# A fused attention and two expert layers on one core: the first loads on two queues, fewer warm products, and another split of the last accumulators

## The chip, the core and the metric

The kernel runs on one core of a Trainium2 chip. A core has TensorE (PE, with its weight loads shown apart as PEld), VectorE (DVE), ScalarE (ACT), GpSimd (POOL) and SyncE (SP), and 16 DMA engines. Here SP and ACT start transfers: SPq and ACTq in the rows below. The metric is the device time of one execution in microseconds (us).

## The reference, cut to what matters

```python
def _attn_ref(q, k, v, tau):            # q, k, v: 4 x 8 x 576 x 64, float32
    scores = scale * np.matmul(q, k.transpose(0, 1, 3, 2))
    thresh = np.max(scores, axis=-1, keepdims=True) - tau
    scores = np.where(scores >= thresh, scores, -1000000000.0)
    ...
    attn = attn / (np.sum(attn, axis=-1, keepdims=True) + 1e-09)
    return np.matmul(attn, v)
# x: the attention's output as 2304 x 512
h = x @ w_in;  r = np.maximum(h, 0.0);  x = (s * (r * r) + b) @ w_out                   # layer one, 512 -> 2048 -> 512
h = x @ w_in;  return (np.maximum(h, 0.0) + alpha * np.minimum(h, 0.0)) @ w_out         # layer two, same sizes
```

## The kernel before, in words

The attention works on pairs of heads: 16 pairs, of which the first four (`p < NP`) are done with plain float32 products and the others with split operands. For each pair, two heads of q, k and v are brought into tiles called `nat` (three of them, used in turn) and `v32`, 128 rows by 4 blocks for the main part of one head (128 KB, the function `load`, L667), and for the last 64 of the 576 rows a small transfer for both heads, the tail (32 KB, L684 and L686). The tail of k and the tail of q of one pair lie in the same tile `nat["k"]`, in its fifth block: k in partitions 0 to 63, q in 64 to 127. PE turns `nat` by transposes (L317 and L319) into a PSUM bank; ACT copies turned k to `k32` (L726), DVE and ACT write the scaled q of either head to `q32` (L738, L740; the first pair's lies in the tile `gw`); PE multiplies them to scores (L804, tile `sc`, two of them); DVE takes the row maximum (L814, `mx`), POOL the threshold (L816), ACT the exponential (L818) and DVE the masked product with its sum (L820, `e`). Then e is turned and multiplied with v.

The order on each engine is not written by hand. Every piece of work is a task with an engine (or several to choose from), a cost, its reads and writes as `Buf` objects, and a rank; `Plan.run` walks through a modelled time and gives each free engine the ready task of lowest rank. What it emits is one fixed list per engine, and the instructions' own semaphore waits are put in afterwards, by tile. So a change of one cost or rank at the start can reorder everything behind it. Layer one is mixed in with the attention by the same ranks; its weights are brought and rebuilt by DVE, ACT and POOL meanwhile. The helpers of its products have the lines L541 to L543, three products for each pair of split operands.

`warm` (L902) adds a product of the identity with itself, which nothing reads. `FILL` is their number ahead of the first transposes, `FILLS` the number behind the first pair's transposes, `FILL1` that behind its first scores.

The value `tau` reaches `tau_b` by the first transfer of ACT's queue (L1042); five small DVE instructions make the scales `sc_p`, `by_half` and the threshold `tau_s` of it.

At the end, layer two's output is made in groups of 128 tokens of two blocks by seven products in the order `TURNS` = (1, 2, 5, 6, 3, 7, 4), each over eight steps (the last step of a group: 7 times 6 products, L541 to L543). Their seven accumulators of 256 columns share four PSUM banks, two and two in that order: (1, 2), (5, 6), (3, 7), (4). DVE and ACT then combine them (L1547, L1553, L1557), and `store` writes out (L1565).

## Time and profile before

| | |
|---|---|
| time, median of 3 runs | 1084.25 us (1083.76 to 1086.61) |
| profiled execution: its own time, its span | 1086.08 us, 1084.3 us |
| PE busy, DVE busy, ACT busy, POOL busy | 1054.1, 918.8, 773.6, 374.0 us |
| instructions | 21629 |
| DMA moved | 175.70 MB, mean 162 GB/s |

The span is that from the first to the last instruction; the execution's own time is 1.8 us longer. Times in the rows below count from the span's start. A row of the timeline gives the start, the duration, the engine, the line, the operation with output and inputs, how many were merged into the row, and in brackets how long the engine had been idle and what ended that. A float32 product counts as two instructions there. A busy PE is not a PE at its peak, since overlapping products are merged.

### The profile page before, as it was taken

To read this page: it belongs to the slowest core of one execution; us is meant where nothing else is said; L and a number is where in the kernel's file an instruction comes from. 1 tells how busy PE (TensorE), PEld (TensorE's weight loads), DVE (VectorE), ACT (ScalarE), POOL (GpSimd) and SP (SyncE) were. 2 spreads that over 40 slices of the span, in tenths; PEclk is the share of its full clock that TensorE was granted. 3 is DMA by queue.
4 is the path that set the end of the run, shared out by engine and by line. 5 is a ranking of instruction groups with operands and counts; after the bars stand their busy time and mean duration, and the time that the engine had idled before them with its cause. 6 is when DMAs were issued, how large, how long until landed. Compare 5 with 4: busy or idle time off the path is not lost.

```text
span 1084.3 us, 21629 instructions
## 1 busy us (share of the span) xinstructions
PE 1054.1 (97%) x7022; PEld 1001.0 (92%) x7022; DVE 918.8 (85%) x2089; ACT 773.6 (71%) x1853; POOL 374.0 (34%) x505
## 2 busy tenths in 40 slices
PE   9999889999999999999999999999999999999998
PEld 8767789999898889989999989999999999999998
DVE  5998978998988898958788897798989999998872
ACT  5888867977887788755656685886968996655550
POOL 1566755654674366520100121150102332112110
PEclk9999999999999999999999999999999999999999
DMA  5874464565546653435446976277785564554531
GB/s 131 234 205 124 133 168 113 136 175 135 126 99 167 159 129 93 123 87 169 152 162 225 307 246 197 77 225 242 243 261 203 168 205 147 160 159 121 147 89 39
DMA packets 198385, 175.70 MB, mean 162 GB/s; under 512 B 73600, under 2 KB 176000, under 8 KB 198272
## 3 DMA queue, kind: packets, MB, share of 16 engines
q1 hardware_dynamic: 195968, 172.69, 54.9%
q10 hardware_dynamic: 2304, 1.64, 0.6%
q8 instruction: 55, 0.90, 0.4%
q14 instruction: 58, 0.48, 0.1%
HBM read 100.54 MB, written 50.86 MB: 140 GB/s over the span
## 4 chain that ended last, share of the span: by engine, by line
PE 78%; DVE 5%; DMA 4%; ACT 3%; issue 2%; POOL 1%; SPq 0%; DVEq 0%; ACTq 0%; POOLq 0%
PE bank L541 13%; PE bank L542 12%; PE bank L543 12%; PE bank_b L541 8%; PE bank_b L542 8%; PE bank_b L543 8%; PE bank L926 6%; PE sc L804 6%; PE bank L319 3%; PE bank L317 3%; DMA stg<-in_moe_w_out_dram 3%; DVE e L820 1%; DMA q<-hq 0%; DMA gf<-gw 0%; DVE mx L814 0%
## 5 line engine op out<-in xcount | busy, mean ns | idle before, releaser
L820 DVE SCALAR_TENSOR_TENSOR e<-sc,mx,e 128x576 f32<-128x576 f32 x144 | 116.3, 812 | 15.6 <-ACT e L818 12.5
L814 DVE TENSOR_REDUCE mx<-sc 128x1 f32<-128x576 f32 x144 | 107.0, 749 | 9.2 <-PE sc L804 8.4
L818 ACT ACTIVATE e<-sc,mx 128x576 f32<-128x576 f32 x144 | 106.1, 742 | 10.3 <-DVE mx L814 9.8
L319 PE MATMUL bank<-eyes_r,e 128*128 128x128 f32 (+1 forms) x320 | 89.3, 286 | 0.3 <-ACT e L818 0.3
L541 PE MATMUL bank<-xt,wa 128*128 128x480 f32 (+3 forms) x224 | 83.2, 372 | 6.4 <-ACT gw L1458 2.2
L541 PE MATMUL bank<-gt,wa 128*128 128x384 f32 (+4 forms) x244 | 84.1, 345 | 2.3 <-DVE wa L472 1.5
L542 PE MATMUL bank<-gt,wa 128*128 128x384 f32 (+4 forms) x244 | 81.6, 334 | 0.0
L543 PE MATMUL bank<-gt,wa 128*128 128x384 f32 (+4 forms) x244 | 81.5, 334 | 0.0
L816 POOL TENSOR_SCALAR mx<-mx,tau_s 128x1 f32<-128x1 f32 x144 | 48.0, 334 | 84.0 <-DVE mx L814 79.4
L542 PE MATMUL bank<-xt,wa 128*128 128x480 f32 (+3 forms) x224 | 75.6, 337 | 0.0
L543 PE MATMUL bank<-xt,wa 128*128 128x480 f32 (+3 forms) x224 | 75.5, 337 | 0.0
L926 PE MATMUL bank<-gl,vt 128*128 128x256 f32 (+1 forms) x192 | 65.0, 339 | 0.0
L926 PE MATMUL bank<-gh,vt 128*128 128x256 f32 (+1 forms) x192 | 57.4, 300 | 0.0
L804 PE MATMUL sc<-k,q 128*128 128x288 f32 x264 | 54.5, 334 | 2.8 <-issue 1.7
L984 DVE TENSOR_TENSOR gl<-bank,gh 128x256 fp32r<-128x256 f32 (+1 forms) x96 | 43.4, 452 | 13.0 <-ACT gh L982 11.7
L541 PEld LDWEIGHTS bank<-xt,wa 128*128 128x128 f32 x224 | 43.0, 192 | 11.6 <-ACT rest L572 2.2
L994 POOL TENSOR_TENSOR gr<-gf,gh 64x256 fp32r<-64x256 f32 (+1 forms) x48 | 40.0, 833 | 38.0 <-DVE gl L992 35.1
L541 PEld LDWEIGHTS bank<-gt,wa 128*128 128x128 f32 x244 | 46.5, 190 | 3.4 <-DVE wa L472 1.7
L319 PEld LDWEIGHTS bank<-eyes_r,e 128*128 128x128 f32 (+1 forms) x320 | 44.5, 139 | 5.1 <-ACT e L818 0.5
L543 PEld LDWEIGHTS bank<-gt,wa 128*128 128x128 f32 x244 | 46.0, 189 | 1.6
L982 ACT ACTIVATE gh<-bank 128x256 fp32r<-128x256 f32 (+1 forms) x96 | 39.4, 410 | 11.0 <-PE bank L319 8.8
L542 PEld LDWEIGHTS bank<-gt,wa 128*128 128x128 f32 x244 | 46.1, 189 | 0.5
(734 smaller groups left out, 4206.2 us busy)
## 6 DMA issues: line engine op xcount, KB each, us to landing
stg<-in_moe_w_in_dram SPq DMA_DIRECT2D x32, 512.0 KB, 4.8
stg<-in_moe_w_out_dram SPq DMA_DIRECT2D x32, 512.0 KB, 4.1
gf<-gw SPq DMA_DIRECT2D x41, 192.0 KB, 2.7
q<-hq SPq DMA_DIRECT2D x24, 256.0 KB, 4.1
qo<-hq SPq DMA_DIRECT2D x24, 256.0 KB, 5.1
gw<-gf SPq DMA_DIRECT2D x48, 128.0 KB, 2.9
xt<-xs SPq DMA_DIRECT2D x13, 384.0 KB, 4.9
yat<-ya SPq DMA_DIRECT2D x24, 192.0 KB, 3.5
```

The costliest lines, as they stand in the source:

```text
L319: nc.tensor.transpose(to, part(x), one)
L541: nc.tensor.matmul(o, lhsT=wl, rhs=mh, start=first, stop=False, skip_group_check=on_top)
L542: nc.tensor.matmul(o, lhsT=wh, rhs=ml, start=False, stop=False, skip_group_check=on_top)
L543: nc.tensor.matmul(o, lhsT=wh, rhs=mh, start=False, stop=last, skip_group_check=on_top)
L804: nc.tensor.matmul(sp.t[:, x, :HS], lhsT=o[0][:, c], rhs=o[1][:, x * HS:(x + 1) * HS], start=n == 0, stop=n == len(passes) - 1)
L814: add("DVE", dve(S), lambda sp=sp, mx=mx: nc.vector.tensor_reduce(mx.t[:, 0:1], sp.t[:, :, :HS], op=ALU.max, axis=AX.XY, negate=True), (sp ...
L816: t2 = add("POOL", 0.26, lambda mx=mx: nc.gpsimd.tensor_scalar(mx.t[:, 1:2], mx.t[:, 0:1], -1.0, tau_s, op0=ALU.mult, op1=ALU.subtract), ( ...
L818: add("ACT", act(S, 1), lambda sp=sp, mx=mx, e=e: nc.scalar.activation(halves(e.t), sp.t[:, :, :HS], AF.Exp, bias=mx.t[:, 0:1]), (sp, mx), ...
L820: add("DVE", dve(S) + 0.065, lambda sp=sp, mx=mx, e=e, col=col, sums=sums: nc.vector.scalar_tensor_tensor(halves(e.t), sp.t[:, :, :HS], mx ...
L926: nc.tensor.matmul(o.t[:, :n], lhsT=w.rearrange("p a b -> p (a b)"), rhs=m.t[:, :n], start=c == first and x == 0, stop=c == last and x == ...
L984: add("DVE", dve(n), lambda hi=hi, lo=lo, gt=gt: nc.vector.tensor_tensor(lo.t[:, :n], gt.t[:, :n], f32(hi.t[:, :n]), op=ALU.subtract), (gt ...
L994: add("POOL", pool2(n), lambda hi=hi, f=f, hf=hf: nc.gpsimd.tensor_tensor(hi.t[:TL, :n], f.t[:TL, :n], f32(hf.t[:TL, :n]), op=ALU.subtract ...
```

## The change

It has three parts. The second heads of the first pair's q and k come by ACT's queue, and with them tau moves: its transfer and its five DVE instructions become tasks, the transfer behind these two heads on ACT's queue; k's tail goes over to SP's queue, q's tail stays on ACT's. The tasks of the two tails write a `Buf` of their own (`ending`), so that in the plan the main transposes don't depend on them. The warm products: `FILL` from 12 to 6, and `FILLS` from 3, 2 and 2 to 1, 0 and 2. And the last group of layer two asks for five banks, with another map of products to banks: (1, 2), (5, 6), (3), (7, 4); the fifth `Buf` gets no product and so no bank.

```diff
-FILL, FILL1 = 12, 3
-FILLS = {("k", False): 3, ("k", True): 2, ("q", False): 2}
+FILL, FILL1 = 6, 3
+FILLS = {("k", False): 1, ("k", True): 0, ("q", False): 2}
...
+        def first_consts():
+            x = add("ACT", 0.4, lambda: nc.scalar.dma_start(tau_b, tau.unsqueeze(0).to_broadcast([P, 1])), rank=-LATER, tail=2.2)
+            of_tau.append(add("DVE", 0.9, scales, after=(x,), rank=-LATER))
...
+                    if p == 0 and nm != "v" and h == 1:
+                        add("ACT", 0.66, lambda t=t, src=src: nc.scalar.dma_start(
+                            t.t[:, 0:NQ, 1, :], src[b, h0 + 1, 0:NQ * P, :].rearrange("(p c) d -> p c d", c=NQ)), (), (t,), (), -LATER, wire=wire(128, 256))
+                        if nm == "q":
+                            first_consts()
+                        continue
...
+            ending = Buf()
...
-                        add("ACT", 0.6, lambda t=t, r=r, tl=tl: nc.scalar.dma_start(t.t[r, NQ], tl), (), (t,), (), -LATER, wire=wire(32, 256))
+                        add("SP" if nm == "k" else "ACT", 0.6, lambda t=t, r=r, tl=tl, e=nc.sync if nm == "k" else nc.scalar: e.dma_start(
+                            t.t[r, NQ], tl), (), (ending,), (), asked[nm] if nm == "k" else -LATER, wire=wire(32, 256))
...
-                            add("PE", turned(len(cs)), transpose, (t,), (tr,) if first else (tr, hl), rank=ready)
+                            add("PE", turned(len(cs)), transpose, (t, ending) if tail else (t,), (tr,) if first else (tr, hl), rank=ready)
...
-                acc = [Buf(moe_s) for _ in range(4)]
+                end = i == len(pairs) - 1 and it == TB // P - 1
+                acc = [Buf(moe_s) for _ in range(4 + end)]
...
-                def at(k, acc=acc):
+                def at(k, acc=acc, end=end):
                     x = TURNS.index(k)
+                    x += end and x > 4
                     return acc[x // 2], slice(x % 2 * G1, x % 2 * G1 + G1)
```

The scaling tasks of q also get `after=of_tau`, and the five DVE instructions move into a function `scales`.

Here are rows of ACT's list at the program's start before the change; nat_135 holds the first pair's k and both its tails.

```order
L1042 DMA tau_b<-in_tau_dram 128x1
L684 DMA nat_135<-in_k_dram 64x2x64
L684 DMA nat_135<-in_q_dram 64x2x64
L726 ACT_TABLE_LOAD
L726 ACTIVATE k_181<-bank_109 128x512
L726 ACTIVATE k_181<-bank_112 128x64
L740 ACTIVATE gw_106<-bank_112,by_half 128x64
L740 ACTIVATE gw_106<-bank_109,by_half 128x256
L740 ACTIVATE gw_106<-bank_111,by_half 128x256
```

The same place of ACT's list in the changed kernel; nat_129 is now the tile of k and the tails, nat_131 that of q.

```order
L677 DMA nat_129<-in_k_dram 128x4x64
L677 DMA nat_131<-in_q_dram 128x4x64
L655 DMA tau_b<-in_tau_dram 128x1
L697 DMA nat_129<-in_q_dram 64x2x64
L740 ACT_TABLE_LOAD
L740 ACTIVATE k_175<-bank_109 128x512
L754 ACTIVATE gw_106<-bank_111,by_half 128x256
L754 ACTIVATE gw_106<-bank_110,by_half 128x256
L740 ACTIVATE k_175<-bank_112 128x64
L754 ACTIVATE gw_106<-bank_112,by_half 128x64
```

Two 128 KB transfers stand ahead of tau and of q's tail, and the copy of k's turned tail has moved behind two of q's scalings.

PE's list before, from the last of the nine warm products to the first score, with the semaphores that a row waits for in brackets (DMAHW1, DMAHW2 and so on are those of single transfers).

```order
L902 MATMUL bank_111<-eyes_r 128x128
L317 MATMUL bank_109<-eyes_r,nat0r 128x128 [waits DMAHW3_49,DMAHW4_49,DMAHW2_49,DMAHW1_49]
L317 MATMUL bank_109<-eyes_r,nat0r 128x128 x2
L319 MATMUL bank_109<-eyes_r,nat_135 128x128
L902 MATMUL bank_110<-eyes_r 128x128
L319 MATMUL bank_112<-eyes_r,nat_135 128x128
L902 MATMUL bank_111<-eyes_r 128x128
L902 MATMUL bank_110<-eyes_r 128x128
L317 MATMUL bank_109<-eyes_r,nat1r 128x128 [waits DMAHW6_49,DMAHW5_49,Activation_49]
...
L902 MATMUL bank_110<-eyes_r 128x128 x2
L804 MATMUL sc_113<-k_181,gw_106 128x288 [waits DVE_49]
L804 MATMUL sc_113<-k_181,gw_106 128x288 [waits Activation_49]
```

And in the changed kernel, from the last of now six warm products.

```order
L916 MATMUL bank_111<-eyes_r 128x128
L317 MATMUL bank_109<-eyes_r,nat0r 128x128 [waits DMAHW5_49,DMAHW6_49,DMAHW1_49,DMAHW0_49]
L317 MATMUL bank_109<-eyes_r,nat0r 128x128 x2
L319 MATMUL bank_109<-eyes_r,nat_129 128x128
L916 MATMUL bank_110<-eyes_r 128x128
L317 MATMUL bank_111<-eyes_r,nat1r 128x128 [waits DMAHW3_49,DMAHW2_49]
...
L916 MATMUL bank_109<-eyes_r 128x128 [waits Activation_49]
L319 MATMUL bank_112<-eyes_r,nat_129 128x128
L916 MATMUL bank_109<-eyes_r 128x128
L818 MATMUL sc_113<-k_175,gw_106 128x288 [waits DVE_49]
L818 MATMUL sc_113<-k_175,gw_106 128x288 [waits Activation_49]
```

The first transposes still wait for four transfers, as before; the tail's transpose has moved behind q's, and three warm products instead of five lie between the first transposes and the first score.

DVE's last rows before the change: the sums of layer two's last group, from the one that reads product 3.

```order
L1553 TENSOR_TENSOR yat_5713<-bank_111,rest_104 128x256 [waits DVE_49,PE_49]
L1553 TENSOR_TENSOR gw_106<-bank_111,rest_104 128x256 [waits Pool_49]
L1557 TENSOR_TENSOR yat_5713<-yat_5713,yb_5716 128x256 [waits DVE_49,Activation_49]
L1553 TENSOR_TENSOR gw_106<-bank_109,gw_106 128x256 [waits DVE_49,PE_49]
L1557 TENSOR_TENSOR yb_5716<-yb_5716,gw_106 128x256 [waits DVE_49]
```

The same rows of the changed kernel.

```order
L1570 TENSOR_TENSOR yat_5694<-bank_112,rest_104 128x256 [waits DVE_49,PE_49]
L1574 TENSOR_TENSOR yat_5694<-yat_5694,yb_5697 128x256 [waits DVE_49,Activation_49]
L1570 TENSOR_TENSOR gw_106<-bank_109,rest_104 128x256 [waits PE_49,Pool_49]
L1574 TENSOR_TENSOR yb_5697<-yb_5697,gw_106 128x256 [waits DVE_49]
L1570 TENSOR_TENSOR gw_106<-bank_109,gw_106 128x256
```

Products 3 and 7 no longer share a bank; 7 and 4 do, one wait serves both of their readers, and two sums have changed places.

## Rows read from the trace of the kernel before

**Rows 1.** Windows: each engine's busy time in a stretch, granted clock, DMA share, GB/s.

```profile
20.00:140.00 120.00, 111.56 (x686) 88.61 (x685) 107.33 (x243) 98.91 (x230) 75.07 (x93) 1.00 0.63 169
140.00:240.00 100.00, 95.42 (x763) 92.75 (x762) 85.13 (x197) 77.69 (x184) 56.60 (x86) 1.00 0.56 146
240.00:480.00 240.00, 236.60 (x1635) 217.38 (x1635) 201.90 (x472) 186.49 (x430) 130.92 (x193) 1.00 0.49 125
900.00:1075.00 175.00, 175.00 (x1462) 175.00 (x1461) 143.45 (x407) 92.97 (x262) 30.06 (x32) 1.00 0.46 128
```

**Rows 2.** Timeline of the start, PE and its weight loads.

```profile
1.62 4.21 PE L902 MATMUL bank<-eyes_r 128*128 128x128 f32 x18 [1.62 <-DVE eyes_r L1040]
...
5.48 0.69 PE L317 MATMUL bank<-eyes_r,nat0r 128*128 128x128 f32 x3
...
6.20 0.64 PE L902 MATMUL bank<-eyes_r 128*128 128x128 f32 x2
...
6.62 0.91 PEld L902 LDWEIGHTS bank<-eyes_r 128*128 128x128 f32 x4
...
7.80 0.53 PEld L902 LDWEIGHTS bank<-eyes_r 128*128 128x128 f32 x4
...
8.55 1.24 PE L804 MATMUL sc<-k,gw 128*128 128x288 f32 x4
...
9.76 0.46 PE L317 MATMUL bank<-eyes_r,nat2r 128*128 128x128 f32 x3
...
10.41 1.14 PE L804 MATMUL sc<-k,gw 128*128 128x288 f32 x4
```

**Rows 3.** Timeline of the start, the queues of SP and ACT.

```profile
0.73 1.36 SPq L667 DMA_DIRECT2D nat<-in_k_dram  x2
0.73 0.39 ACTq L1042 DMA_DIRECT2D tau_b<-in_tau_dram  x1
...
1.93 0.64 ACTq L684 DMA_DIRECT2D nat<-in_q_dram  x1
```

**Rows 4.** DMA issues of 0.5 to 2.05 us: count, KB each, median us to landing.

```profile
nat<-in_k_dram SPq DMA_DIRECT2D x2, 128.0 KB, 3.3
nat<-in_k_dram ACTq DMA_DIRECT2D x1, 32.0 KB, 3.1
nat<-in_q_dram ACTq DMA_DIRECT2D x1, 32.0 KB, 3.1
```

**Rows 5.** DMA view of 0 to 20 us: GB/s in 40 slices of 0.5 us.

```profile
GB/s 0 0 0 0 28 99 247 245 208 227 241 197 172 109 65 43 223 72 218 224 187 142 109 162 124 201 114 161 222 93 62 217 165 127 155 158 194 57 63 26
```

**Rows 6.** Timeline of the start, DVE and ACT.

```profile
8.01 0.48 DVE L738 TENSOR_SCALAR gw<-bank,by_half 128x256 f32<-128x256 f32 x1 [0.64 <-PE bank L319]
8.53 0.84 ACT L740 ACTIVATE gw<-bank,by_half 128x256 f32<-128x256 f32 x2 [0.70 <-DVE gw L738]
...
11.58 0.76 DVE L814 TENSOR_REDUCE mx<-sc 128x1 f32<-128x576 f32 x1 [1.00 <-PE sc L804]
...
11.91 0.22 ACT L726 ACTIVATE k<-bank 128x64 f32<-128x64 f32 x1 [0.30 <-PE bank L319]
```

**Rows 7.** Waits of PE, 20 to 480 us: total us, times, longest.

```profile
PE bank L541 <- ACT rest L572: 2.0, 5, 0.7
...
PE bank L319 <- DVE z L877: 0.2, 1, 0.2
```

**Rows 8.** Timeline of the end, DVE, PE and ACT's queue.

```profile
1079.14 0.42 DVE L1553 TENSOR_TENSOR yat<-bank,rest 128x256 f32<-128x256 f32 x1 [1.02 <-PE bank L543]
...
1079.42 0.28 PE L542 MATMUL bank<-wa,xt 128*128 128x256 f32 x1
1079.54 0.28 PE L543 MATMUL bank<-wa,xt 128*128 128x256 f32 x1
...
1080.48 0.41 DVE L1557 TENSOR_TENSOR yb<-yb,gw 128x256 f32<-128x256 f32 x1
...
1080.92 0.72 ACTq L1565 DMA_DIRECT2D out_dram<-yb  x1
```

## What the change was predicted to do

> **What bounds the kernel now.** I read the windows first, to see where an earlier or later start could matter and where nothing but PE counts. From 240 us on PE is busy for 236.6 of 240 us, and near the end for 175 of 175 [rows 1]: there its work fixes the time. Before, it isn't so: from 20 to 140 us PE has 8.4 us of gaps and DVE is at 107.3 of 120, from 140 to 240 PE has 4.6 us of gaps. Together with the 3.4 us of the third row that is 16.4 us of idle PE ahead of 480 us, and it is all that another order can win. The list of PE's waits shows no single cause in them: 18 kinds, 32 waits, from 2.0 us in total down to 0.2 us, by ACT, DVE and DMA in turn [rows 7].
>
> Then I read the timeline of the first 12 us. PE runs nine warm products from 1.62 us, turns k from about 5.4, and begins the first score at 8.55, the second at 10.41 [rows 2]. DVE's maximum of the second score starts at 11.58, having waited 1.00 us for PE [rows 6]. What follows hangs on it: DVE is one list, and its first masked product stands behind this maximum. So I measure the start by this point, and not by the first score.
>
> **What the first transposes wait for.** The plan now frees k's main transposes from the tails, but the list doesn't: the row of the first transpose still waits for four transfers, k's two heads and both tails, since the tails are issued ahead of it into the same tile. Before, the heads were issued at 0.73 and, half of the merged 1.36 us later, at 1.41 [rows 3], and landed 3.3 us on [rows 4], at 4.0 and 4.7; q's tail was issued at 1.93 and landed at 5.0. The nine warm products took PE to 5.4, at 0.42 us each (18 instructions up to there), and covered it all.
>
> In the changed kernel k's second head comes earlier, but q's tail, the last of the four, is ACT's fourth transfer: 0.73 + 2 x 0.68 for the two heads + 0.39 for tau = 2.5 us, and 3.1 us to landing gives 5.6 as the lower bound. The upper one is the rate. Two queues now push k, q and the tails, 4 x 128 + 2 x 32 KB = 590,000 bytes, and the tails stand last in both. The queues had moved 64,000 bytes by 3.0 us and then 208 to 247 GB/s, 234 in the mean to 5.5 us [rows 5]; the other 526,000 take 2.25 us, to 5.25. From the move to the landing it was at most 0.9 us before: the 328,000 bytes of k and its tails were through by 4.1 us at the earliest, and landed by 5.0. That ends at 6.1. I take 5.9, nearer to the rate, which the slices show to be flat with one queue already. So the first transposes come 0.5 us later than at 5.4, although only six warm products stand ahead, which end at 1.62 + 6 x 0.42 = 4.1; PE idles 1.8 us in between.
>
> The Trainium skill (DMA: Bandwidth & Descriptors, "Issuing engines are not separate DMA queues") says that transfers started by different engines run on the same 16 DMA engines and interleave; by it the second queue would save only time of issue. The flat 234 GB/s agrees with that.
>
> **From there to the second score.** How fast PE works then is open. Until about 7.4 us the same four weight loads of warm products take 0.91 us, at 7.80 they take 0.53 [rows 2]: PE starts at 1.2 GHz and had been busy without a break since 1.62 when it came to 2.4 GHz (the column of the granted clock shows 1.00 all along, the durations show the step). I bound it from both sides.
>
> Full rate from 7.4 on, as before: k's transposes from 5.9 to 6.6 (0.72 before, from 5.48 to 6.20), one warm product to 7.05, q's four transposes and a warm product to 7.9, the tail's to 8.05, a warm product to 8.3. DVE scales q from 7.6 to 8.1 (0.48), and the first half of the first score can run at 8.3. The second half needs the last columns of k, and their copy has moved on ACT behind two scalings of q (0.84 for two), of which the first waits for DVE: 8.1 + 0.9 + 0.22 [rows 6] = 9.25. So the first score ends at 9.9, where it ended at 9.79 before. The next transposes need the bank of q's tail: DVE's second scaling (0.48, behind ACT's on the same bank) ends at 9.5, and the tail's 64 columns, on DVE and then on ACT, each about the 0.22 of k's, at 10.1. Then the transposes, 0.46; the second score, 1.14: its maximum at 11.8. That is 0.2 us later than 11.58. The saved warm products (two lay between the scores before) are in this sum, and pay for most of what the late tail costs.
>
> 1.2 GHz until PE has been busy again as long as it was from 1.62 to 7.4, that is till 11.7: transposes and warm products to 9.0 instead of 8.3, the first score takes 2.2 instead of 1.14 and ends at 11.2, the next transposes at 11.7, the second score at full rate to 12.9. That is 1.3 us later. I take 0.8, since the new idle 1.8 us lies just ahead of the work; bounds 0.2 and 1.3. It passes on to the end in full, I take it, because DVE has its steady work right behind; were it all lost in DVE's 12.7 us of gaps up to 140 us [rows 1], it would be 0, so the start's term lies between 0 and 1.3.
>
> The Trainium skill (TensorE: Matmul & The Clock Gate, "What's actually happening") says that the throttled clock is the default and that activity releases it. By it fewer warm products and a gap are a price, and the upper bound is the likelier one: 0.5 us more than I take. The step from 0.91 to 0.53 agrees with it.
>
> **tau.** Its transfer stands behind two heads, and its five DVE instructions ahead of q's scaling, which can start at 7.6. It lands ahead of q's tail in the same queue, by 5.8, and five instructions of one to four columns each take less than the 0.41 us of 256 columns [rows 8]: done by 7.85 at the latest. So it costs between 0 and 0.25, and I take 0, since they are far smaller than that row. V's and the second pair's loads slide about 1 us on SP's queue and are needed from 10 us on: nothing.
>
> **The end.** A step of the last group is 7 x 6 products of 0.12 us (1079.42 to 1079.54), and the last product ends at 1079.8. Before, the sum with product 3 started at 1079.14, with the end of product 7, which shares its bank [rows 8]. Now it starts with its own end, twelve products before the last, at 1078.4, and its store goes 0.9 us earlier. But product 7's reader now waits for product 4, at 1079.86, and two sums follow at 0.33 us each: the last begins at 1080.53, where it began at 1080.48. The last store follows it at once, as at 1080.92. So 0.05 us are lost, and the two last stores have the queues more to themselves: 0.0, between -0.3 and +0.1.
>
> **The order between.** From layer one's second part on PE's rows are the same, but about half of all rows ahead of it stand elsewhere. The counts on each engine differ by a few: by eight at most for one line, with as many the other way on the next line, out of 1947 rows of DVE; I take nothing for that. Each of the 32 waits (0.5 us in the mean) is drawn anew. If each moves by its own size, that is 0.5 x the root of 32 = 2.8 us; DVE's steady work evens part of it out, so 0 with about 2 either way.
>
> **Sum.** The profiled execution took 1086.08 us, 1084.3 of span and 1.8 around it; 1086.08 + 0.8 + 0.0 + 0 = 1086.9. The median is 1.83 lower: 1085.0.
>
> **Rivals.**
> 1. The heads do come early: the two tails get through between the heads, the first transposes start at 4.6 rather than 5.9 (as the plan means it), with the clock up at 7.4. Then the start is 1.3 us better than the 0.2 of the full rate: 1.1 won, 1083.15. For it: the heads themselves are in by 4.5. Against it: 5.6 by issue alone.
> 2. The other side: PE stays at 1.2 GHz through the first pair. The score of 1.14 us takes 2.2, at every one of the next scores, and from 11.7 on each us at the low clock costs 0.5. It decides if the clock isn't up by 15.6: 1.3 + 2.0 = 3.3 us, so 1087.6 and more. For it: PE's work has short gaps now, with four warm products fewer among the scores. Against it: from 8.55 to 11.55 the two scores and the transposes leave PE hardly 0.2 us free before [rows 2], and in the new list they stand as close.
> 3. The new order closes gaps: a quarter of the 16.4 us is 4: 1081.0.
> 4. It opens as many: 1088.5.
>
> **Chances.** The forecast 0.52, with 1083.0 to 1087.0 as its own range; rival 1 0.18; rival 2 0.08; rivals 3 and 4 0.11 each. What a measurement tells from no change is 0.3%, 3.25 us: under 1081.0 or over 1087.5. Faster: 0.06 of rival 3, 0.04 of rival 1 and the forecast with a lucky order: 0.10. Slower: 0.05 of rival 2, 0.08 of rival 4: 0.13. The rest, 0.77, is the same. The range 1081.8 to 1088.0 leaves out most of rivals 3 and 4 and half of 2, 0.19.
>
> **What would show it.** First transposes at 5.6 to 6.1 and a gap of PE ahead of them from 4.1; weight loads of 0.23 us after 7.4; the first score's second half waiting for ACT; the second maximum between 11.8 and 12.9. In the end, the sum with product 3 at 1078.4 and the last sum at 1080.5 relative to the same last product. Gaps of PE from 20 to 480 us between 14 and 19. The prediction is wrong if the first transposes start before 5.4, or if that idle time moves by more than 3 us.

## The result and the profile after

The changed kernel takes 1093.95 us (median of four runs, 1092.58 to 1094.16), beside 1084.01 of the kernel before (four runs too): a ratio of 1.0084, 95% interval 1.0066 to 1.0102. It is 0.84% slower, and above the predicted range of 1081.8 to 1088.0. The profiled execution took 1094.16 us, with a span of 1092.4; before these were 1086.08 and 1084.3.

The windows after, which answer to [rows 1]:

```profile
20.00:140.00 120.00, 108.59 (x650) 86.47 (x648) 108.62 (x233) 96.45 (x222) 74.79 (x88) 0.97 0.61 166
140.00:240.00 100.00, 96.80 (x757) 92.44 (x758) 82.92 (x196) 78.19 (x188) 56.18 (x85) 1.00 0.54 139
240.00:480.00 240.00, 236.43 (x1632) 215.78 (x1631) 201.97 (x479) 187.57 (x427) 133.53 (x198) 1.00 0.51 130
```

Only the first row has changed much: from 20 to 140 us PE is 3 us less busy, its granted clock is no longer 1.00, and it did 650 instructions instead of 686.

The timeline of the start, all engines, against [rows 2, 3, 6]:

```profile
2.12 0.64 ACTq L655 DMA_DIRECT2D tau_b<-in_tau_dram  x1
2.79 0.64 ACTq L697 DMA_DIRECT2D nat<-in_q_dram  x1
...
3.08 1.31 SPq L673 DMA_DIRECT2D nat<-in_k_dram  x2
...
6.38 0.59 PE L317 MATMUL bank<-eyes_r,nat0r 128*128 128x128 f32 x3 [1.83 <-DMA nat<-in_q_dram]
...
6.50 0.21 DVE L1065 TENSOR_SCALAR tau_s<-tau_b,lost 128x1 f32<-128x1 f32 x1
...
9.14 2.13 PE L818 MATMUL sc<-k,gw 128*128 128x288 f32 x4
9.24 0.23 ACT L740 ACTIVATE k<-bank 128x64 f32<-128x64 f32 x1
...
10.58 0.23 PEld L317 LDWEIGHTS bank<-eyes_r,nat2r 128*128 128x128 f32 x1
...
11.63 1.50 PE L818 MATMUL sc<-k,gw 128*128 128x288 f32 x4
...
12.73 0.15 PEld L319 LDWEIGHTS bank<-eyes_r,nat 128*128 128x128 f32 x1
13.17 0.76 DVE L828 TENSOR_REDUCE mx<-sc 128x1 f32<-128x576 f32 x1 [1.11 <-PE sc L818]
```

The first transposes wait for q's tail, as predicted, and weight loads stay at 0.23 us until past 10.6, so PE was at 1.2 GHz through both transposes and the first score. The second score's maximum comes at 13.17 instead of 11.58: 1.59 us later.

PE's waits from 20 to 480 us, the three largest kinds of 14 (total, times, longest), against [rows 7]:

```profile
PE bank L541 <- ACT rest L572: 4.4, 10, 0.6
PE bank L317 <- DVE e L834: 3.0, 2, 2.8
PE sc L818 <- DVE e L834: 2.4, 3, 1.4
```

All of them come to 17.3 us in 30 waits, where they were 16.1 in 32. By this sum next to nothing has happened. But one wait of 2.8 us is new. The timeline around it, POOL, DVE and PE:

```profile
60.74 1.52 POOL L472 TENSOR_TENSOR wa<-n,wa 128x512 fp32r<-128x512 f32 x1
61.06 1.76 DVE L434 SCALAR_TENSOR_TENSOR n<-stg,n 128x512 int32<-128x512 int32 x1
...
61.51 0.30 PE L317 MATMUL bank<-eyes_r,e5r 128*128 128x128 f32 x1
...
63.74 0.80 DVE L834 SCALAR_TENSOR_TENSOR e<-sc,mx,e 128x576 f32<-128x576 f32 x1
...
64.61 0.37 PE L317 MATMUL bank<-eyes_r,e0r 128*128 128x128 f32 x1 [2.79 <-DVE e L834]
```

And the windows of the same microseconds (PE's busy time first, the granted clock third from the end):

```profile
62.00:64.00 2.00, 0.00 (x0) 0.00 (x0) 2.00 (x4) 0.82 (x3) 0.35 (x2) 0.89 0.03 3
64.00:66.00 2.00, 1.40 (x8) 1.40 (x9) 1.89 (x5) 1.99 (x5) 2.00 (x3) 0.50 0.84 236
66.00:68.00 2.00, 2.00 (x9) 1.48 (x9) 1.35 (x5) 1.64 (x5) 0.64 (x3) 0.50 1.02 281
68.00:70.00 2.00, 2.00 (x6) 1.46 (x6) 2.00 (x3) 1.62 (x4) 1.37 (x2) 0.50 0.76 158
```

DVE's instruction of line 434 takes 1.76 us, 0.69 elsewhere, beside POOL's subtraction (line 472), which ends 0.56 us before it. That POOL holds it up is a guess here; runs 15 to 18 go into it. The mask behind it is late, PE waits, and behind the wait PE's granted clock is 0.50, which is 1.2 GHz, until 70 us.

The end, DVE, PE and ACT's queue, against [rows 8]:

```profile
1086.81 0.42 DVE L1570 TENSOR_TENSOR yat<-bank,rest 128x256 f32<-128x256 f32 x1 [0.30 <-PE bank L543]
1087.92 0.28 PE L543 MATMUL bank<-wa,xt 128*128 128x256 f32 x1
1089.11 0.41 DVE L1570 TENSOR_TENSOR gw<-bank,gw 128x256 f32<-128x256 f32 x1
1089.60 0.34 ACTq L1582 DMA_DIRECT2D out_dram<-gw  x1
```

The last product starts 8.38 us later than before (1079.54), the span ends 8.1 later: the end gained 0.28 us. DVE's list is the same in both kernels from about 530 us on, and its instructions stand 8.4 us later at 531 as at 1056. So all was lost ahead of 530 us.

**Where, by equal work.** A sum of waits in a fixed window can't show it, since the later kernel does less work in the window. So I counted the columns of PE's products, instruction by instruction (a float32 product is two instructions; warm products are left out), and looked when each kernel had done what before had done by 20, 100, 140, 240, 400 and 500 us. At 531 us this count makes the changed kernel 8.5 us late, where DVE's rows say 8.4. It has its noise all the same: run 3 below, with before's order on another chip, takes 2.2 us more than before from 140 to 240 us, and 0.5 or less in each of the other stretches. Duration of a stretch, and PE's waits in it:

```text
                 0-20       20-100      100-140    140-240     240-400     400-500
before         19.9/1.9    80.1/4.4    40.0/3.8   100.0/4.5   159.9/3.2   100.0/0.2
after          20.9/3.6    84.5/8.1    39.3/3.2   101.1/2.7   159.6/1.8   103.3/2.2
```

Two stretches lose most: 4.4 us from 20 to 100, 3.3 from 400 to 500; the start loses 1.0. (The expectations of runs 13 to 18 say 6 and 3.6 us for the two stretches; they go by a coarser count, of merged rows.) The second shows as PE waiting for ACT's reads of the hidden banks:

```profile
PE bank L541 <- ACT rest L572: 1.2, 3, 0.5
PE bank L541 <- ACT rest L1098: 1.0, 2, 0.8
```

These are all of PE's waits from 400 to 505 us; before there was a single one:

```profile
PE bank L541 <- ACT rest L1083: 0.2, 1, 0.2
```

The rows of waits understate them, since they count from the modelled end of the product before. One of them in the timeline of PE, after:

```profile
441.80 0.29 PE L319 MATMUL bank<-eyes_r,nat 128*128 128x128 f32 x1
442.41 0.49 PE L541 MATMUL bank<-xt,wa 128*128 128x480 f32 x1 [0.32 <-ACT rest L572]
```

The two starts are 0.61 us apart, where the same pair without a wait has 0.03 to 0.06, so this wait of 0.32 costs 0.55 us. Counted so, from start to start, the five waits of the rows and a sixth that is too short for them cost 3.7 us after, and the single one 0.3 before: that is the whole loss of this stretch.

### The profile page after: what moved, and what is told of

Read it like the earlier page. It is cut to its first block, busy times and chain, and to the rows that moved or that the text cites. A ratio compares the mean times of both kernels' runs of the same rounds, so it can differ in the third digit from the quotient of the medians.

```text
span 1092.4 us, 21566 instructions
## 1 busy us (share of the span) xinstructions
PE 1057.6 (97%) x7002; PEld 1001.9 (92%) x7002; DVE 917.9 (84%) x2094; ACT 774.8 (71%) x1850; POOL 376.2 (34%) x503
## 4 chain that ended last, share of the span: by engine, by line
PE 76%; DVE 9%; ACT 6%; DMA 5%; issue 3%; POOL 0%; ACTq 0%; SPq 0%; DVEq 0%
PE bank L541 12%; PE bank L542 11%; PE bank L543 11%; PE bank L940 7%; PE sc L818 7%; PE bank_b L541 7%; PE bank_b L542 7%; PE bank_b L543 7%; PE bank L319 4%; PE bank L317 3%; DMA stg<-in_moe_w_out_dram 2%; ACT e L832 1%; DVE e L834 1%; DVE mx L828 1%; DVE yb L1221 1%
## 5 line engine op out<-in xcount | busy, mean ns | idle before, releaser
L996 ACT ACTIVATE gh<-bank 128x256 fp32r<-128x256 f32 (+1 forms) x96 | 39.3, 410 | 19.5 <-PE bank L319 17.3
L541 PEld LDWEIGHTS bank<-gt,wa 128*128 128x128 f32 x244 | 46.4, 190 | 2.5 <-ACT rest L1098 1.1
L993 POOL TENSOR_TENSOR gl<-gf,gh 128x256 fp32r<-128x256 f32 (+1 forms) x48 | 39.2, 816 | 24.6 <-DVE gh L992 14.4
L543 PEld LDWEIGHTS bank<-gt,wa 128*128 128x128 f32 x244 | 45.9, 188 | 1.7
```

Of the source, the lines that this page charges most:

```text
L541: nc.tensor.matmul(o, lhsT=wl, rhs=mh, start=first, stop=False, skip_group_check=on_top)
L543: nc.tensor.matmul(o, lhsT=wh, rhs=mh, start=False, stop=last, skip_group_check=on_top)
L996: add("ACT", act(n), lambda hi=hi, gt=gt: nc.scalar.activation(hi.t[:, :n], gt.t[:, :n], AF.Copy), (gt,), (hi,), rank=rank)
```

## The experiments

Each ratio is to runs of the kernel before on the same chip; on these chips before took 1087.8 to 1088.5 us in the median, 4 us more than on the first, so ratios are compared and not times. Theory A: the new list costs. Theory B: the late start throws the rest out of step. More theories come below, where they arose. Times by equal work are from one profiled execution of each run.

**1. The new start in the old order.** Before's plan; the real transfers, the five DVE instructions and the number of real warm products are the new ones.

```diff
+                        (nc.scalar if p == 0 and nm != "v" and h else nc.sync).dma_start(
...
+            add("PE", 0.28, lambda: real and nc.tensor.matmul(
```

> The list of before on every engine, row by row, with the changed start put into it: second heads and tau on ACT's queue, k's tail on SP's, ten warm products fewer. The accumulators of the end are as before. Theory A, the new list is what costs: only the start is lost, the second maximum comes 1 to 2 us later, and the time is 1085 to 1086.5. Theory B, the late start and the slow clock throw all that follows out of step, whatever the list: 1090 or more.

Measured: 1.001 (0.9992 to 1.0028).

```profile
6.55 0.60 PE L317 MATMUL bank<-eyes_r,nat0r 128*128 128x128 f32 x3 [1.99 <-DMA nat<-in_q_dram]
...
13.39 0.76 DVE L826 TENSOR_REDUCE mx<-sc 128x1 f32<-128x576 f32 x1 [0.99 <-PE sc L816]
```

The start is even 1.81 us later at the second maximum, and 1.1 us of that reach the end (-0.9 to 3.0, so zero isn't excluded). Theory B, with 1090 or more, falls.

**2. The old start in the new order.** The reverse: after's plan, before's transfers, tau and warm products.

```diff
-                        add("ACT", 0.66, lambda t=t, src=src: nc.scalar.dma_start(
+                        add("ACT", 0.66, lambda t=t, src=src: nc.sync.dma_start(
```

> The list of the changed kernel on every engine, row by row, with the start of before put into it: heads on SP's queue, tau and both tails ahead on ACT's, nine warm products ahead of the first transposes. Theory A: the start's 1.6 us come back and the rest stays, 1091 to 1093. Theory B: the loss goes with the start, 1083 to 1086.

Measured: 1.0057 (1.004 to 1.0075), though the second maximum comes at 10.98 us, earlier than in either kernel.

```profile
10.98 0.76 DVE L828 TENSOR_REDUCE mx<-sc 128x1 f32<-128x576 f32 x1 [0.99 <-PE sc L818]
```

The list costs 6 us by itself.

**3. The new bank map alone**, in the kernel before.

```diff
+                end = i == len(pairs) - 1 and it == TB // P - 1
+                acc = [Buf(moe_s) for _ in range(4 + end)]
...
+                    x += end and x > 4
```

> Before with the other map of the last group's products to banks alone. Both theories expect next to nothing: the last sum 0.25 us later against the last product, the end of the span 0.3 us earlier, so 1083.5 to 1084.2 beside 1084.0. A rival for the end, that the bank is worth more than that, expects under 1083.

Measured: 0.9998 (0.9984 to 1.0012). The fifth bank is worth nothing that this run can tell, within 1.7 us either way.

**4. The tails in a tile of their own**, so that the heads are early in fact.

```diff
-                            t.t[r, NQ], tl), (), (ending,)
+                            endt[r], tl), (), (ending,)
```

> The changed kernel with the first pair's tails in a tile of their own, so that the first transposes wait for k's two heads alone; the list is that of the changed kernel. If the four-transfer wait is the cause of the late start, the first transposes come at 4.7 to 5.2 instead of 6.35 and the second maximum 1 to 2 us earlier. Theory A: 1091.5 to 1093. Theory B, or a list that fits the early start it was planned for: under 1087.

Measured: 1.0058 (1.0037 to 1.0079).

```profile
4.21 0.69 PE L317 MATMUL bank<-eyes_r,nat0r 128*128 128x128 f32 x3
...
11.13 0.76 DVE L832 TENSOR_REDUCE mx<-sc 128x1 f32<-128x576 f32 x1 [0.99 <-PE sc L822]
```

The first transposes come even earlier than the 4.7 to 5.2 that were expected. The second maximum is 2.04 us earlier than in the changed kernel and 0.45 earlier than before, and the kernel is still 0.6% slower. Theory B falls here too.

**5 to 8. Other lists with the same instructions.** One number of the plan is changed and nothing real. Two with the old start, a warm product planned at 0.34 or 0.22 us; two with the new, tau's landing planned at 2.6 or 3.8.

```diff
-            add("PE", 0.28, lambda: nc.tensor.matmul(w.t[:, :P], lhsT=ident,
+            add("PE", 0.34, lambda: nc.tensor.matmul(w.t[:, :P], lhsT=ident,
...
-to_broadcast([P, 1])), rank=-LATER, tail=2.2)
+to_broadcast([P, 1])), rank=-LATER, tail=2.6)
```

> The kernel before with one number of its plan changed: a warm product is planned at 0.34 us instead of 0.28, so that the order on every engine comes out another way (3,860 of PE's rows stand elsewhere) while every instruction, transfer and the start stay what they were. Theory A, that a list is a draw and costs of several us come and go with it: the ratio to before leaves 0.998 to 1.002, and most likely upward (1.002 to 1.008), since before's list has few gaps. Theory A2, that only the new list has something bad in it: 0.999 to 1.001. PE's waits from 20 to 480 us tell: 16.1 us before; 1 us more time should go with 1 us more of them, or with granted clock lost.

> The same with a warm product planned at 0.22 us: another order again (3,714 of PE's rows elsewhere), the same instructions and start. Theory A: a ratio of its own, 1.002 to 1.008 or 0.996, not that of the first; theory A2: 0.999 to 1.001.

> The changed kernel with tau's landing planned 2.6 us behind its issue instead of 2.2: the same instructions and the same start, another order behind it (4,500 of PE's rows elsewhere). Theory A: a ratio to before that differs from the changed kernel's 1.006 to 1.008 by 2 us or more (below 1.004 or above 1.010). Theory A3, that the late start itself makes any list behind it slow: 1.005 to 1.009 as the changed kernel.

> The same with tau's landing planned 3.8 us behind its issue: a third order behind the new start. Theory A: again a ratio of its own, 1.000 to 1.010; theory A3: 1.005 to 1.009.

Measured: 1.0025 (1.0007 to 1.0042), 1.0048 (1.003 to 1.0066), 1.0083 (1.0062 to 1.0104), 1.007 (1.0044 to 1.0096). All four are slower than before. PE's largest wait from 20 to 100 us in the second of them is of the same kind as in the changed kernel, though nothing of the change is in it:

```profile
PE bank L317 <- DVE e L820: 3.2, 1, 3.2
```

So theory A2, that only the new list is bad, falls. The sign that was named for theory A, that PE's waits from 20 to 480 us go with the time, failed: they are 16.1 us in run 5 and 14.5 in run 6, beside 16.1 before. The two with the new start both lie in A3's interval, the first against A's; but A3, that a late start makes any list slow, falls by run 1 (late start, old list, 1.001), and run 4 (early start, new list, 1.0058) shows that a list can be slow without it.

**9. The changed kernel again**, for the chip of the next two.

> The changed kernel itself once more, on the chip of the three runs below, as their measure. Every theory: a ratio of 1.006 to 1.010 to before.

Measured: 1.0065 (1.0043 to 1.0087). In its trace PE's wait for e in the same place is 2.3 us, and the granted clock is 0.50 from 64 to 66 us, 0.65 to 68 and 1.00 from there.

**10. Products in the gap at 61 us**, to hold the clock up (theory C).

```diff
+                        for _ in range(12):
+                            nc.tensor.matmul(gt.t[:, :P], lhsT=ident, rhs=ident, start=True, stop=True)
```

> The changed kernel with twelve identity products on PE ahead of the transposes of e that wait 2.79 us at 64.6 us; nothing else moves, and the products' results are overwritten by those transposes. Theory C, that the clock's fall behind this gap is what costs: the granted clock stays near 1.00 from 64 to 72 us, PE's next work is done in half the time there, and the time falls by 2 to 4 us against the changed kernel. Theory A, that the gaps themselves cost and the clock only a part: at most 1.6 us less (what the spread of 1092.58 to 1094.16 with the granted clock, 0.999 to 0.996, allows).

Measured: 1.0049 (1.0031 to 1.0066); 2.2 us less than run 9 in the median, 1.7 by the ratios, and their intervals overlap. The clock did stay up:

```profile
62.00:64.00 2.00, 2.00 (x21) 2.00 (x19) 2.00 (x4) 1.24 (x3) 0.51 (x2) 1.00 0.17 32
64.00:66.00 2.00, 2.00 (x17) 1.63 (x16) 2.00 (x6) 2.00 (x6) 1.72 (x2) 1.00 0.97 272
66.00:68.00 2.00, 2.00 (x11) 1.38 (x10) 2.00 (x5) 1.69 (x6) 1.62 (x2) 1.00 1.01 274
```

By equal work the stretch from 20 to 100 us takes 83.5 us, 85.2 in run 9. So the fall of the clock is about a quarter of the loss of 7.8 us on this chip. That lies between what the two theories had, and the intervals allow nothing as well as more than that.

**11. DVE's long instruction moved behind the mask** (theory D: DVE is full there, and the gap comes back).

```diff
+                        if t.mark == "or" and self.ors in LATE_OR:
+                            self.late[LATE_OR[self.ors]] = t
```

> The changed kernel with one DVE instruction moved, its line 434's at 61.06 us, that took 1.76 us (0.69 elsewhere) while POOL ran a tensor_tensor: it stands behind the second next mask now, by 63.7 us. Theory A, that the list's order on DVE is what makes PE wait: PE's wait of 2.79 us at 64.6 falls below 1 us, the clock does not fall there, and the time falls by 2 to 4 us against the changed kernel. Theory D, that DVE is full in this stretch, so that a gap taken away here comes back at the next mask: the same time within 1 us, with the waits for e at 80 to 90 us longer.

Measured: 1.0065 (1.0044 to 1.0086), as run 9.

```profile
62.09 0.28 PE L331 MATMUL bank<-eyes_r,e0r 128*128 128x128 f32 x1 [0.75 <-DVE e L849]
...
63.08 0.69 DVE L448 SCALAR_TENSOR_TENSOR n<-stg,n 128x512 int32<-128x512 int32 x1 [1.05 <-DMA stg<-in_moe_w_in_dram]
...
64.43 0.38 PE L333 MATMUL bank<-eyes_r,nat 128*128 128x128 f32 x1 [1.14 <-DVE hk L776]
...
66.53 1.55 DVE L448 SCALAR_TENSOR_TENSOR n<-stg,n 128x512 int32<-128x512 int32 x1
```

```profile
66.00:68.00 2.00, 2.00 (x6) 1.46 (x6) 1.96 (x4) 2.00 (x6) 1.54 (x2) 0.50 0.46 122
```

The first fence is the timeline of PE and DVE, the second a window. The wait is down to 0.75 us, the next one comes 2.3 us later, and the clock falls behind that. Theory A's gain does not come; the time is the one that theory D named: the largest wait was a place where the lateness showed, and not its cause. D's reason isn't shown, though. The waits for e at 80 to 90 us are no longer (1.3 us, 1.4 in run 9), and DVE isn't full here: it waits 1.05 us for a transfer at 63.08. And the next instruction of the same line (L448 here) takes 1.55 us at 66.53.

**12. Everything early in the old order**: runs 1 and 3 together, with the tails in their own tile as in run 4.

> The order of before on every engine, the second heads and tau on ACT's queue, ten warm products fewer, the fifth bank, and the two tails in a tile of their own, so that the first transposes wait for k's two heads alone. In that order the tail's transpose stands right behind k's, so PE gets on only with the tails. Theory A, that with the order of before the start is worth what it moves: first transposes at 4.2 instead of 5.4 us, the second maximum 0 to 1.5 us later than 11.58, and a ratio of 0.999 to 1.002. Theory B, that an early start of the transposes is worth its 1.2 us: 0.998 to 0.9995.

Measured: 0.9993 (0.9969 to 1.0017). The first transposes come at 4.21 and the second maximum at 12.35, inside theory A's range. With the old list the change's parts are worth nothing that can be told from zero; the interval allows 3.4 us won and 1.8 lost.

**13, 14. Re-planned late.** One DVE instruction planned 0.5 us longer at 270 us, in before and in the changed kernel. Theory E: the first 100 us decide; F: the stretch from 400 to 500.

```diff
+                        if now > 270.0 and e == "DVE" and not self.late:
+                            us += 0.5
+                            self.late = True
```

> The kernel before with its plan disturbed at 270 us of planned time alone (one DVE instruction planned 0.5 us longer): the rows ahead of that stand as they stood, those from there to about 500 us come out another way (1,082 of PE's rows). Theory E, that the list of the first 100 us is where the new order loses: ratio 0.999 to 1.002. Theory F, that the stretch from 400 to 500 us decides, since what is lost ahead of it is made up: 1.002 to 1.005, with waits of PE for ACT's rest in that stretch (0.2 us in before).

> The changed kernel with the same disturbance at 270 us: its first 270 us stay as they were. By equal work of PE the stretch from 400 to 500 us takes 103.7 us in the changed kernel and 100.1 in before; another draw of it should take 100 to 103.7. Theory E: a ratio of 1.004 to 1.009, since the 6 us of the first stretch stay. Theory F: 1.000 to 1.004 if the new draw has no waits for ACT's rest there.

Measured: 1.0018 (1.0001 to 1.0035) and 1.0089 (1.0056 to 1.0122). Both ratios lie in theory E's ranges. But before's first stretch stays good (80.4 us by equal work) and its stretch from 400 to 500 becomes 102.5 us with 1.9 of waits, as theory F had it, and the time grows by about that much; in the other, the first stays bad (85.2) and the new draw of the late one is hardly better (102.6). Neither theory alone: both stretches count, each with its own part.

**15 to 18. POOL's subtraction cut short**, in the two orders (theory H: DVE and POOL hold one another up). First with the tiles' second parts set to zero by POOL, then by DVE, since POOL's zeroing held tau's DVE instructions (last section).

```diff
-                part(1), n3(), f32(part(0)), op=ALU.subtract)
+                part(1)[:, :1], n3()[:, :1], f32(part(0))[:, :1], op=ALU.subtract) if e == "POOL" else ...
```

> The kernel before, every instruction in its old place but for POOL's, with POOL's subtraction for the weights' second parts (line 472) on a quarter of its columns, so that the rest of those parts is left out, and the ten weight tiles' second parts set to zero at the start by POOL. The partner of the next: the time itself matters less than the difference of the two. 0 to 6 us less than before, plus up to 2 us for the start.

> The changed kernel with the same cut of POOL's subtraction and the same part left out. Theory H, that the new order loses by DVE and POOL holding one another up: the difference to its partner in the order of before falls from 7 to 9 us to 4 or less, and DVE's held time from 20 to 140 us comes to the same in both. Theory A without H, that the order loses in other waits: the difference stays at 6 to 9 us.

> The kernel before with POOL's subtraction for the weights' second parts on a quarter of its columns (the rest left out), and these parts set to zero by DVE from 1.6 us on, in its idle time. The partner of the next. 0.995 to 1.001 of before.

> The changed kernel with the same cut and the same part left out. Theory H, DVE and POOL hold one another up in the first 100 us: what the order loses up to 100 us, 6 us by equal work of PE, falls to 2 or less, the 3.6 us from 400 to 500 us stay, and the difference of the two times is 3 to 5 us. Theory A without H: 6 us stay in the first stretch and the difference is 7 to 9.

Measured: 1.0041 (1.0021 to 1.0062) and 1.0081 (1.0052 to 1.011); then 1.0061 (1.004 to 1.0083) and 1.009 (1.0074 to 1.0107). All four do the work of before's first 20 us some 5 to 7 us late, so their own levels say nothing, and runs 15 and 17 missed what was expected of them by themselves. In the first pair the medians differ by 5.95 us, which is neither theory's; the ratios differ by 0.40% with about 0.36 either way: it decides nothing. In the second, with equal starts (tau's first DVE instruction at 12.31 us in both) and five rounds, the medians differ by 3.5 us, the ratios by 0.29% with about 0.27 either way. By equal work, from 20 to 100 and from 400 to 500 us, with DVE's held time in the first of the two (each DVE instruction's time above the time that the quickest fifth of its form stays within):

```text
                                  20-100   held   400-500
before                             80.1     4.1    100.0
old order, POOL cut (15, 17)       79.9     3.9     99.8
                                   80.1     4.2    100.1
after                              84.5     9.1    103.3
new order, POOL cut (16, 18)       81.9     6.1    103.4
                                   81.9     6.1    103.3
other lists: 5, 6                  84.5     6.4    102.0
                                   85.2     8.9    103.3
             7, 8                  86.1     8.5    102.6
                                   86.6     8.1     99.9
old order: runs 1, 3, 12        79.7-80.6 3.9-4.2    100.0
old to 270 us, 13                  80.4     3.4    102.5
```

With POOL cut short, what the new order loses from 20 to 100 us falls from 4.4 to 2.0 and 1.8 (theory H had 2 or less), and from 400 to 500 3.6 and 3.2 stay of 3.3, as it said. That the held time comes to the same in both orders, as run 16 had it for theory H, it does not: 6.1 and 4. The means of lines 434 and 428 from 20 to 140 us in before, in the changed kernel, and in the changed kernel with POOL cut (run 18, where they are lines 435 and 429):

```profile
L434 DVE SCALAR_TENSOR_TENSOR n<-stg,n 128x512 int32<-128x512 int32 x20 | 14.3, 713 | 0.0
L428 DVE TENSOR_SCALAR n<-stg 128x512 f32<-128x512 f32 x5 | 2.1, 423 | 0.7 <-POOL wa L472 0.7
```

```profile
L434 DVE SCALAR_TENSOR_TENSOR n<-stg,n 128x512 int32<-128x512 int32 x20 | 16.5, 824 | 0.0
L428 DVE TENSOR_SCALAR n<-stg 128x512 f32<-128x512 f32 x6 | 4.8, 794 | 0.0
```

```profile
L435 DVE SCALAR_TENSOR_TENSOR n<-stg,n 128x512 int32<-128x512 int32 x20 | 14.2, 708 | 0.0
L429 DVE TENSOR_SCALAR n<-stg 128x512 f32<-128x512 f32 x6 | 4.5, 744 | 0.0
```

Line 434's extra time goes with the cut; line 428's stays. The cut also takes work from POOL, so the hold and POOL's own lateness aren't parted. So POOL's subtraction carries more than half of the first stretch's loss in the new order; that it does so by holding DVE up fits the held times, which are 6.4 to 9.1 in all five slow lists and 3.4 to 4.2 in before's, but isn't shown. Run 5 loses 4.4 us with only 2.3 more of held time.

## Why the prediction was wrong, step by step

**What bounds the kernel.** Right: the larger part of the loss fell where PE has gaps [rows 1]. Missed: from 400 to 500 us PE had 0.2 us of waits, and 3.3 us were lost there all the same. A stretch without gaps can gain nothing from a new order; it can lose.

**The first transposes.** Right in what they wait for, 0.5 us short in when: 6.38 for 5.9, above the bound of 6.1. Tau's issue took 0.64 us behind the two heads, not 0.39, so that q's tail was issued at 2.79, and the transposes began 3.6 us behind that, not 3.1. The bound from the rate counted six transfers; SP's queue issued the second pair's k from 3.08 on, and whether that held the tail up was not tried.

**The second maximum.** 13.17, above the range of 11.8 to 12.9. Of the two branches the upper one came true, PE at 1.2 GHz past 10.6 us; its 12.9 and the late 0.5 make 13.4, 0.2 more than measured. I had taken a value between the two; the rule of the Trainium skill (TensorE: Matmul & The Clock Gate, "What's actually happening") had pointed to the upper one, and the weight loads of 0.23 us agree with it. To the end the start costs 1.1 us (run 1: -0.9 to 3.0), where 0.8 was in the sum: that term holds.

**tau.** Right: done by 6.71, ahead of DVE's first scaling at 8.00.

**The end.** Right at 0.0: 0.28 gained in the trace, 0.9998 in run 3. The last sum came 0.25 us later behind the last product, not 0.05, and the last store took 0.34 instead of 0.72.

**The order between.** This is the step that failed: "If each moves by its own size, that is 0.5 x the root of 32 = 2.8 us; DVE's steady work evens part of it out, so 0 with about 2 either way." In its place the runs show 6 us lost with the old start (run 2) and 6 to 8 with the new. Rival 4, the same mechanism with a quarter of the gaps, had 0.11 and 1088.5 (1089.0 by its own 4 us on the forecast): too small as well. Two things were wrong in it.

First, the mean. A list drawn anew doesn't scatter around before's. Seven other lists were run (the changed kernel's, runs 5 to 8, 13 and 14) and all seven are slower, by 0.18 to 0.89%, 0.6% in the mean; none is faster. They aren't all independent: run 13 keeps before's list up to 270 us, run 14 the changed kernel's. Before's list is the best of the eight: little held time of DVE in the first 100 us, and from 400 to 500 us one wait of 0.2. From such a place every change of order that was tried made the kernel slower, and by these lists the term would have been about +6 with 3 either way. Why before's list is so good no run shows.

Second, the measure. I priced the redrawing by PE's waits. From 20 to 480 us they went from 16.1 to 17.3, inside the 14 to 19 that I had named as the sign of being right, while the time went up by 8. By equal work the waits of the two bad stretches grew by 5.7 us, those from 140 to 400 shrank by 3.2. And a row of waits is less than what the wait costs: from 400 to 500 us they grew by 2.0, and from start to start by 3.4. From 20 to 100 us PE also worked at 0.50 of its clock for 6 us.

**The rivals.** The first, early heads, did not happen, and run 4 shows that it would have won nothing in this list. The second, the low clock through the first pair, came only to 12 us. But the clock did fall later, behind the wait that began at 61.8 us, which no term of the sum had; run 10 prices that at about 2 us, with zero not excluded.

**What is shown and what is argued.** Shown: the list costs 6 us with the old start (run 2) and 6 to 8 with the new one (the changed kernel beside run 1); the start about 1, with zero not excluded; the end nothing that could be told. By the traces most of the loss lies in two stretches, which run 13 moves apart, and cutting POOL's subtraction takes more than half of the first away and nothing of the second. Argued: that the first is POOL holding DVE up; and that the second is ACT's lateness in reading hidden banks, which the trace shows at each of its waits, but no run changed. What makes ACT late there, and what the rest of the first stretch is, stays open.

## What to carry to other kernels

Where a planner makes the order, price a re-plan before anything else, by disturbing one harmless cost in the plan: two such lists cost here 0.25 and 0.48% with no change of the work, more than any other term of the change. Where a kernel's list is the best of several, as here, an edit at the start that draws it anew loses in the mean, and not by chance alone; if the edit is wanted, keep the list (run 12 does, at 0.9993) or draw several. And compare two kernels at equal work: waits summed in a fixed window hid 8 us.

## What the runs showed of the hardware

A DVE instruction can stand not for one POOL instruction but for a whole run of them. In run 15 DVE's scaling of two columns, 0.23 us long elsewhere, stood from 3.81 to 11.86:

```profile
1.68 8.95 POOL L1051 MEMSET wa<- 128x1024 f32 x10
...
3.55 0.15 DVE L1046 TENSOR_SCALAR sc_p<-keep 128x1 f32<-128x1 f32 x1
3.81 8.05 DVE L1052 TENSOR_SCALAR by_half<-by_half,sc_p 128x2 f32<-128x2 f32 x1
...
11.16 0.68 POOL L621 MEMSET sh<- 128x320 f32 x2
```

It ended when the last of fourteen memsets that follow one another without a gap had ended, at 11.84, 0.06 us before POOL's next one began. Two instructions of one column had passed just ahead of it, beside the same memsets. Run 16 shows it again, with 5.69 us. The Trainium skill (SBUF — State Buffer, "Who interferes with whom") says that DVE and GpSimd share one pair of ports as an exclusive lock, taken by whoever comes first for a whole instruction. The 1.76 us at 61.06 agree with that; that DVE gets no turn between POOL's instructions, as in these two runs, goes beyond it.

And behind a wait of PE of 2.8 us in the middle of the kernel the granted clock was 0.50, 1.2 GHz, from 64 to 70 us; behind 2.3 us in run 9 it was back at 1.00 by 68; and with twelve products that nobody reads in the place of that wait (run 10) it stayed at 1.00, 2.4 GHz.
